# An eight-expert layer with its routing computed during the work: rows' transposes on more PSUM buffers, constant products in the first expert's waits, a fifth raw weight buffer, low parts of weights ahead of routing, and other modelled latencies for the second routing

## The chip, the cores and the metric

One core of a Trainium2 chip. The time is the device time of one execution in microseconds. The kernel before ran three times: 911.78, 912.67 and 908.16, median 911.78. The profile is of a further execution that took 908.89, with a span of 907.0 from its first to its last instruction.

## What is computed

An attention of 4 x 8 heads over 576 positions (windowed in half of the heads, dilated in the others) gives x, 2304 rows of 512. Two layers of experts follow, each with 8 experts of 512 x 1024 and 1024 x 512 weights. All inputs and the output are float32.

```
# first layer: a row goes to one expert, experts take at most 288 rows, best scores first
cap = N // E
for idx in np.argsort(-(x @ w_gate).flatten()):
    tok, e = idx // E, idx % E
    if assigned[tok] >= 0 or counts[e] >= cap: continue
    assigned[tok] = e; counts[e] += 1
for e in range(E): out[mask] = np.maximum(x[mask] @ w1[e], 0.0) @ w2[e]
# second layer: noisy gate, the two best experts of each row, their outputs weighted and summed
noisy_logits = logits + np.log1p(np.exp(x @ w_noise)) * noise
out[mask] += top2_w[mask, k] * (np.maximum(x[mask] @ w1[e], 0.0) @ w2[e])
```

The first layer's assignment is a sequential rule, so the kernel finds one expert's rows after another: it fixes the experts in the order in which they fill, and while it computes expert k it works out who goes to expert k+1 and those behind it.

## The kernel before, in words

**Number format.** Every float32 product of the experts is three products of rounded parts: high x high, low x high, high x low (`mm3`, the line L786). ScalarE rounds an operand to its high part, VectorE subtracts to get the low part. For weights that is `split` (ScalarE `whi` L747 of 128 x 1024, VectorE `wlo` L751 in two halves of 512), for rows `split_x` (`xh` L769, `xl` L770), for the hidden layer `split_h` (`hh` L773, `hl` L774).

**An expert of the first layer.** Its routing list is turned into row numbers (L701 on TensorE, `cp` and `idx` on VectorE). GpSimd gathers 3 x 96 rows `g` from `xr`, the copy of x in DRAM (`gather1`, L796). `tx1` transposes the rows in four groups of three (L810, tiles of the PSUM pool `tr`, which has two buffers) and splits each group into `xh` and `xl`: the third group can't start before the first group's `xl` is out of its buffer. `ffn1` then makes 8 blocks of 12 products (128 x 288 each) for the hidden layer and 4 blocks of 24 for the output: 192 products an expert. After an expert, `post1` computes the second layer's gate from its output (L848), transposes the output back (L867) and writes it to the second layer's x.

**Weights** stream in chunks of 512 KB into the pool `rp` of 4 raw buffers (SyncE issues, L729 for the first matrix, L739 for the second); a raw buffer comes free when the last `wlo` half is subtracted. `load()` issues a chunk when fewer than 4 lie between loaded and split.

**Routing** is a Python generator (`routing`, L451 to L633). For an expert it makes two or three searches for a threshold: VectorE `I` (L540, thresholds against scores), TensorE `OH` products (L558), VectorE `sat` (L560), a small product (L569), `w` (L573); then `choices` (some 20 small VectorE instructions, L491 to L511) and the list. In this text "the sat" is L560.

**The order.** Engines work in program order, and Python sets that order in `build()`: a planner walks through the 192 products of each expert and keeps modelled clocks, `self.pe` for TensorE, `self.dv` for VectorE and `self.tR` for the routing's next TensorE step. `step()` emits the routing's next piece, `spend(t)` advances over a product and emits what has become due, `idle()` emits what is next where the first expert has nothing to compute. `shade(dur)` emits, while VectorE would wait for the routing's answer, what fits: pending `hl` (`self.work`), then low parts of weights through `lows(t, end)`, then routing work of a later expert. `later` holds `hl` back, `flush` empties the queue.

**First expert.** `rows` (L440) transposes x itself, 18 blocks of 128 rows with four transposes each (L446), through the same two `tr` buffers, ScalarE copies the block (L448), SyncE writes it to `xr`. `ROWS0` says how many blocks stand between the routing's steps.

**Second routing.** `noisy` (L879) finds the two best experts of 18 columns of rows: MAX and index instructions in three groups of six (L909, L911), the exponential of the weights on ScalarE (L920, behind a table load), scans (L924), prefix products on TensorE (L928 to L930, called NOISY here), and more VectorE work. `slots` (L991) then builds the list of rows: R (L1014), A (L1023) on VectorE, and products on TensorE (L1028, called SLOT); `gather2` and `tx2` (L1060) bring the rows. It runs once in expert 6 for the rows of experts 0 to 5, and once in the first expert of the second layer.

The calls that matter, with the part that fixes a position: at the end of each first-layer expert `build` finishes what is left of the previous one's `tail`, and for expert 6 that tail holds NOISY and SLOT:

```
                if tail:
                    finish(tail)
                tail = self.post1(k)
                if k == E - 3:
                    tail = itertools.chain(tail, self.noisy(0, NA), first())
```

Of the kernel before, what the change touches and what calls it, by code (L numbers as in the profile page):

```python
# [9 lines left out]
F32 = mybir.dt.float32  # L10
# [14 lines left out]
GB = 96  # L25
# [5 lines left out]
CAP2 = CB * 128  # L31
SEGS = ((0, 256), (256, 384))
# [15 lines left out]
ROWS0 = {False: (6, 1, 3, 1, 3, 1, 3), True: (4, 1, 2, 1, 2, 1, 2, 1, 2, 1, 1)}  # L48
# [97 lines left out]
class Body:  # L146
# [281 lines left out]
    def open_moe(self):  # L428
        tc = self.tc
        self.wp = self.ctx.enter_context(tc.tile_pool(name="wp", bufs=10))  # L430
        self.rp = self.ctx.enter_context(tc.tile_pool(name="rp", bufs=4))
        self.gp = self.ctx.enter_context(tc.tile_pool(name="gp", bufs=5))
        self.yp = self.ctx.enter_context(tc.tile_pool(name="yp", bufs=3))
        self.wk = self.ctx.enter_context(tc.tile_pool(name="wk", bufs=1))
        self.w2 = self.ctx.enter_context(tc.tile_pool(name="w2", bufs=2))
        self.mm = self.ctx.enter_context(tc.tile_pool(name="mm", bufs=4, space=PSUM))
        self.tr = self.ctx.enter_context(tc.tile_pool(name="tr", bufs=2, space=PSUM))
        self.rt = self.ctx.enter_context(tc.tile_pool(name="rt", bufs=2, space=PSUM))

    def rows(self, x0T, c0, c1, psum, name, pool):  # L440

        nc = self.nc
        for c in range(c0, c1):
            ps = psum.tile([128, 512], F32, name=name)
            for kk in range(4):
                nc.tensor.transpose(ps[:, kk * 128:(kk + 1) * 128], x0T[kk][:, c * 128:(c + 1) * 128], self.ident)  # L446
            r = pool.tile([128, XW], F32, name="g")
            nc.scalar.activation(r[:, :DM], ps, AF.Copy)  # L448
            nc.sync.dma_start(self.xr[c * 128:(c + 1) * 128, :DM], r[:, :DM])

    def routing(self):  # L451
# [82 lines left out]
        for k in range(E - 1):  # L534
# [54 lines left out]
            if listed:  # L589

                emit = self.lister(k, place(pk), True)
                while self.low:
                    t, f = self.low.pop(0)
                    f()
                    self.chain(t + 0.05)
                yield "pe", k, 0.85
                emit()
                self.chain(0.4)
            choices()
# [41 lines left out]
    def shade(self, dur):  # L641

        end = max(self.rdy, self.pe) + dur + HOP[1] + SLACK[self.lead > 1]
        for q in (self.work, None, self.low):
            if q is None:
                self.lows(self.dv, end)
                continue
# [5 lines left out]
    def later(self, t, f):  # L653
# [5 lines left out]
        while len(self.work) > 2:  # L659
            t, f = self.work.pop(0)  # L660
            f()
            self.dv = max(self.dv, self.pe) + t

# [215 lines left out]
    def noisy(self, c0, c1):  # L879
# [27 lines left out]
        for j0 in range(0, n, 6):  # L907
# [4 lines left out]
            yield 0.0, 0.16 * (min(n, j0 + 6) - j0) + 0.4  # L912
# [6 lines left out]
        yield 0.0, 1.6  # L919
        nc.scalar.activation(ww, ww, AF.Exp)  # L920
# [4 lines left out]
        yield 0.0, max(3.0, 1.2 + 0.08 * n)  # L925
# [4 lines left out]
        nc.tensor.matmul(pr[:GB, 256:256 + E], self.ones[:GB, :GB], S[:, n - 1, :], start=True, stop=True)  # L930
        V.tensor_tensor(sw[:, :, 0], ww[:, :, 0], ww[:, :, 1], op=OP.add)
# [33 lines left out]
    def ranks(self, e0, e1):  # L965
# [5 lines left out]
        t = wk.tile([GB, NCOL, E], F32, name="rkt")[:, :, :e1 - e0]  # L971
# [3 lines left out]
        nm = wk.tile([GB, NCOL, E], F32, name="nm")[:, :, :e1 - e0]  # L975
# [127 lines left out]
    def build(self):  # L1103
# [18 lines left out]
        self.pend = []  # L1122

# [53 lines left out]
        def idle():  # L1177

            task = min(bg, key=lambda x: x[0], default=None)
            if task and task[0] <= self.tR:  # L1180
# [35 lines left out]
        def load():  # L1216

            while len(raw) < min(len(self.W) + 4, len(chunks)) and known(len(raw)):
# [30 lines left out]
        for n in ROWS0[self.exact]:  # L1249
            step()  # L1250
            self.rows(x0T, c, c + n, self.tr, "t", self.gp)
            c += n
        assert 0 in experts and c == NT
        load()
        split(1)
        until(ready, 0)
        split(4)
        while self.tR < ready[0]:
            idle()
        tx = start(self.tx1(0))  # L1260
# [223 lines left out]
```

## Time and profile before

| what | value |
|---|---|
| median of 3 runs | 911.78 us (908.16 to 912.67) |
| the profiled execution | 908.89 us, span 907.0 us |
| TensorE (PE) busy | 838.4 us, 92% |
| VectorE (DVE) busy | 518.9 us, 57% |
| ScalarE (ACT) busy | 366.7 us, 40% |
| GpSimd (POOL) busy | 183.6 us, 20% |
| chain of work that ended last | PE 72%, DVE 14%, DMA 5% |
| mean granted TensorE clock | 0.968 |

In rows of the timeline the columns are: start in us, duration in us, engine, line, operation, output<-inputs, partitions x elements and type, number of instructions merged; in brackets the idle time of the engine ahead of it and what released it. A granted clock of 1.00 is 2.4 GHz, 0.50 is 1.2 GHz.

### The profile page before, as it was taken

What the parts mean: (1) busy time and instruction counts of PE and PEld (TensorE: products, weight loads), DVE (VectorE), ACT (ScalarE), POOL (GpSimd) and SP (SyncE); (2) the same over time, 40 slices, a digit from 0 to 9 for tenths busy, and PEclk for the clock granted to TensorE, in tenths of its full rate; (3) what the DMA queues carried; (4) which work ended last, traced back from release to release, by engine and by line L of the source; (5) the groups of instructions that cost most, each with busy time, mean ns of one, the idle gap of its engine ahead of it and who ended that gap; (6) DMA issues with size and microseconds to landing.
All of it is one profiled execution on the core that took longest, in us unless ns stands there. A gap on an engine that the chain in (4) does not pass through costs nothing.

```text
span 907.0 us, 16969 instructions
## 1 busy us (share of the span) xinstructions
PE 838.4 (92%) x6723; PEld 760.1 (84%) x6725; DVE 518.9 (57%) x1540; ACT 366.7 (40%) x669; POOL 183.6 (20%) x154
## 2 busy tenths in 40 slices
PE   6888678889999999799899999999999999999993
PEld 3666578789888999799788989889899898998982
DVE  5986668678997654964675627336364372552300
ACT  1767543444345465365134334334333333433210
POOL 3875101010112100010131220322212222122011
PEclk9999869899999999899999999999999999999997
DMA  9960745356556854365335453644545445343112
GB/s 315 305 182 3 290 132 175 94 164 208 143 193 187 290 146 164 102 192 163 84 66 178 126 110 92 165 92 127 128 94 159 69 137 144 74 152 47 14 24 38
DMA packets 54521, 126.26 MB, mean 139 GB/s; under 512 B 7712, under 2 KB 8992, under 8 KB 53664
## 3 DMA queue, kind: packets, MB, share of 16 engines
q1 hardware_dynamic: 40960, 94.46, 32.6%
q0 software_dynamic: 10496, 25.77, 14.7%
q10 hardware_dynamic: 2976, 4.85, 1.7%
q8 instruction: 55, 0.90, 0.4%
q14 instruction: 34, 0.28, 0.1%
HBM read 100.42 MB, written 24.72 MB: 138 GB/s over the span
## 4 chain that ended last, share of the span: by engine, by line
PE 72%; DVE 14%; DMA 5%; issue 3%; ACT 3%; POOL 1%; ACTq 0%; SPq 0%; POOLq 0%; DVEq 0%
PE m L786 60%; DVE wlo L751 3%; PE o L302 2%; PE t L1060 2%; PE r L558 2%; PE ps L283 1%; DMA g<-xr,idx 1%; DVE hl L774 1%; DVE R L695 1%; DMA raw<-in_w2a_dram 1%; DMA ct<-in_consts_dram 1%; PE t L810 1%; PE t L446 1%; PE s L251 1%; PE t L848 1%
## 5 line engine op out<-in xcount | busy, mean ns | idle before, releaser
L786 PE MATMUL m<-xh,whi 128*128 128x384 f32 (+2 forms) x768 | 237.9, 310 | 0.4 <-DVE hl L774 0.4
L786 PE MATMUL m<-xl,whi 128*128 128x384 f32 (+2 forms) x768 | 236.6, 308 | 0.0
L786 PE MATMUL m<-xh,wlo 128*128 128x384 f32 (+2 forms) x768 | 236.5, 308 | 0.0
L751 DVE TENSOR_TENSOR wlo<-raw,whi 128x512 fp32r<-128x512 f32 x256 | 163.7, 683 | 51.6 <-ACT whi L747 51.4
L774 DVE SCALAR_TENSOR_TENSOR hl<-m,hh 128x256 fp32r<-128x256 f32 (+2 forms) x192 | 89.7, 474 | 150.0 <-ACT hh L773 149.9
L773 ACT ACTIVATE hh<-m 128x256 fp32r<-128x256 f32 (+2 forms) x192 | 81.5, 427 | 178.9 <-PE m L786 175.1
L786 PEld LDWEIGHTS m<-xl,whi 128*128 128x128 f32 x768 | 146.7, 191 | 4.0 <-issue 3.7
L747 ACT ACTIVATE whi<-raw 128x1024 fp32r<-128x1024 f32 x128 | 134.4, 1053 | 36.3 <-DMA raw<-in_w1a_dram 11.0
L786 PEld LDWEIGHTS m<-xh,whi 128*128 128x128 f32 x768 | 146.7, 191 | 1.0 <-DVE hl L774 0.6
L786 PEld LDWEIGHTS m<-xh,wlo 128*128 128x128 f32 x768 | 146.3, 191 | 0.5 <-issue 0.5
L786 PE MATMUL m<-whi,hl 128*128 128x512 f32 x320 | 129.1, 403 | 0.5 <-DVE hl L774 0.5
L786 PE MATMUL m<-wlo,hh 128*128 128x512 f32 x320 | 125.5, 392 | 0.0
L786 PE MATMUL m<-whi,hh 128*128 128x512 f32 x320 | 125.3, 392 | 0.0
L1097 POOL DMA_INDIRECT out_dram<-y,tk x40 | 64.0, 1600 | 277.7 <-ACT y L1096 255.0
L1096 ACT ACTIVATE y<-m,wte 128x512 f32<-128x512 f32 x40 | 27.5, 688 | 144.6 <-issue 93.9
L770 DVE TENSOR_TENSOR xl<-t,xh 128x512 fp32r<-128x512 f32 (+1 forms) x72 | 41.8, 586 | 72.9 <-ACT xh L769 72.7
L786 PE MATMUL m<-hl,whi 128*128 128x288 f32 x256 | 79.9, 312 | 2.6 <-DVE hl L774 2.5
L786 PE MATMUL m<-hh,whi 128*128 128x288 f32 x256 | 79.0, 308 | 3.5 <-DVE hl L774 3.5
L786 PE MATMUL m<-hh,wlo 128*128 128x288 f32 x256 | 78.6, 307 | 0.0
L1046 POOL DMA_INDIRECT g<-x,pos x40 | 38.8, 971 | 177.8 <-issue 125.3
L786 PEld LDWEIGHTS m<-wlo,hh 128*128 128x128 f32 x320 | 60.5, 189 | 12.6
L786 PEld LDWEIGHTS m<-whi,hl 128*128 128x128 f32 x320 | 60.6, 189 | 12.5 <-DVE hl L774 1.4
(219 smaller groups left out, 1068.2 us busy)
## 6 DMA issues: line engine op xcount, KB each, us to landing
raw<-in_w1a_dram SPq DMA_DIRECT2D x32, 512.0 KB, 4.4
raw<-in_w2a_dram SPq DMA_DIRECT2D x32, 512.0 KB, 3.9
raw<-in_w1b_dram SPq DMA_DIRECT2D x32, 512.0 KB, 4.4
raw<-in_w2b_dram SPq DMA_DIRECT2D x32, 512.0 KB, 3.7
qt<-in_q_dram SPq DMA_DIRECT2D x8, 576.0 KB, 7.5
kt<-in_k_dram SPq DMA_DIRECT2D x8, 576.0 KB, 8.3
xr<-g SPq DMA_DIRECT2D x18, 256.0 KB, 2.6
x<-y ACTq DMA_DIRECT2D x24, 192.0 KB, 2.2
```

Source lines behind the costliest of these rows:

```text
L302: nc.tensor.matmul(o[r, jj * 64:(jj + 1) * 64], VT[g][:, j, hh * 64:hh * 64 + 64], sb[:, a, half(h ^ i)], start=True, stop=True)
L558: nc.tensor.matmul(pc[:, :E], I[:, :, c], OH[:, c, :], start=c == 0, stop=c == NT - 1)
L747: nc.scalar.activation(hi, raw, AF.Copy)
L751: self.pend.append((chunk, self.pe + LOW[0], lambda s=s: nc.vector.tensor_tensor(lo[:, s], raw[:, s], hi[:, s].bitcast(F32), op=OP.subtract)))
L770: self.nc.vector.tensor_tensor(xl, ps, xh.bitcast(F32), op=OP.subtract)
L773: self.nc.scalar.activation(hh, ps, AF.Relu)
L774: self.later(0.4, lambda: self.nc.vector.scalar_tensor_tensor(hl, ps, 0.0, hh.bitcast(F32), op0=OP.max, op1=OP.subtract))
L786: self.nc.tensor.matmul(ps, a, b, start=i == 0, stop=i == n - 1)
L1046: nc.gpsimd.indirect_dma_start(out=g[:, :DM], out_offset=None, in_=self.x1[:rows, :], in_offset=bass.IndirectOffsetOnAxis(ap=pos[:, b:b + ...
L1060: nc.tensor.transpose(ps[:, kk * 128:(kk + 1) * 128], g[:, kk * 128:(kk + 1) * 128], self.ident)
L1096: nc.scalar.activation(y, ps, AF.Copy, scale=wt[:, b:b + 1])
L1097: nc.gpsimd.indirect_dma_start(out=self.out, out_offset=bass.IndirectOffsetOnAxis(ap=tok[:, b:b + 1], axis=0), in_=y, in_offset=None, comp ...
```

## The change

It has six parts. (1) `rows` takes its PSUM tiles from the four-buffer pool `mm` for two blocks of three and from `tr` for the third, and `ROWS0` deals the blocks out as 3, 1, 4, 1, 4, 1, 4 instead of 6, 1, 3, 1, 3, 1, 3. (2) `fill` issues products of the constant table `thr` (128 x 512, bf16) to a PSUM tile that nobody reads, where the planner sees TensorE wait in the first expert; the order has 5 of them ahead of the first prefix products (L519), 13 ahead of the first list's products (L701), 15 ahead of the search behind it (L558), and 5 ahead of the first `tx1`. (3) `rp` has 5 buffers instead of 4, and `load` runs one chunk further ahead; the tiles `rkt` and `nm` share the buffers of `x1T` and `gp`. (4) Pending `hl` are emitted ahead of `choices`. (5) In `shade`, where the routing is two experts ahead or more, every low part whose high part is due by then is emitted, not only what fits into the wait. (6) In `noisy` the modelled latency of a MAX group is 0.6 per column instead of 0.16, that of the scans 2.8 + 0.08 per column, and the exponential stands behind the prefix products, with a latency of 1.8 of its own.

```
-ROWS0 = {False: (6, 1, 3, 1, 3, 1, 3), ...}
+ROWS0 = {False: (3, 1, 4, 1, 4, 1, 4), ...}
-        self.rp = self.ctx.enter_context(tc.tile_pool(name="rp", bufs=4))
+        self.rp = self.ctx.enter_context(tc.tile_pool(name="rp", bufs=RAW))      # RAW = 5
...
-            ps = psum.tile([128, 512], F32, name=name)
+            ps = self.mm.tile([128, 512], F32, name="m") if c % 3 else self.tr.tile([128, 512], F32, name="t")
...
+            self.flush(False)
             choices()
...
-                self.lows(self.dv, end)
+                self.lows(self.dv, end if self.lead < 2 else 1e9)
...
+    def fill(self, t):
+        n = int(0.8 * min(t, 8.0) / 0.225)
+        if n > 1:
+            x = self.thr.rearrange("p a c -> p (a c)")
+            ps = self.mm.tile([128, 512], F32, name="m")
+            for _ in range(n):
+                self.nc.tensor.matmul(ps, x[:, :128], x[:, :512], start=True, stop=True)
...
-            yield 0.0, 0.16 * (min(n, j0 + 6) - j0) + 0.4
+            yield 0.0, 0.6 * (min(n, j0 + 6) - j0) + 0.4
...
-        yield 0.0, 1.6
-        nc.scalar.activation(ww, ww, AF.Exp)
...
-        yield 0.0, max(3.0, 1.2 + 0.08 * n)
+        yield 0.0, 2.8 + 0.08 * n
         pr = self.rt.tile([128, 512], F32, name="r")
...
+        nc.scalar.activation(ww, ww, AF.Exp)
+        yield 0.1, 1.8
         V.tensor_tensor(sw[:, :, 0], ww[:, :, 0], ww[:, :, 1], op=OP.add)
...
-        t = wk.tile([GB, NCOL, E], F32, name="rkt")[:, :, :e1 - e0]
+        t = wk.tile([GB, NCOL, E], F32, name="rkt", tag="x1T")[:, :, :e1 - e0]
-        nm = wk.tile([GB, NCOL, E], F32, name="nm")[:, :, :e1 - e0]
+        nm = wk.tile([GB, NCOL, E], F32, name="nm", tag="gp")[:, :, :e1 - e0]
...
         def idle():
             task = min(bg, key=lambda x: x[0], default=None)
+            if self.cold:
+                self.fill(min(self.tR, task[0] if task else 1e9) - self.pe)
...
-            while len(raw) < min(len(self.W) + 4, len(chunks)) and known(len(raw)):
+            while len(raw) < min(len(self.W) + RAW, len(chunks)) and known(len(raw)):
...
+        self.cold = not self.exact
...
+        if self.cold:
+            self.fill(ready[0] - self.pe)
+            self.cold = False
```

Because the planner's clocks move, so do instructions of all experts. Where a step stands among TensorE's expert products, as expert.product (0.182 is the 182nd of expert 0's 192; experts 8 and on are the second layer's), counted from the order before and now:

| step | before | now |
|---|---|---|
| tx1 of expert 1, first group | 0.182 | 0.182 |
| last sat's OH products, then tx1, for expert 2 | 1.118, 1.130 | 1.149, 1.165 |
| the same for expert 3 | 2.136, 2.158 | 2.104, 2.113 |
| the same for expert 4 | 3.51, 3.97 | 3.71, 3.97 |
| list products, then tx1, for expert 3 | 2.115, 2.158 | 2.63, 2.113 |
| list products, then tx1, for expert 5 | 4.12 (searches done), 4.97 | 4.65, 4.117 |
| NOISY, SLOT in expert 6 | 6.117, 6.190 | 6.174, 7.0 |
| NOISY, SLOT in the second layer's first expert | 8.67, 8.125 | 8.75, 8.139 |
| SLOT in the second layer's next expert, its tx2 | 9.51, 9.83 | 9.47, 9.83 |

(The row for expert 5 before names the list of expert 5 itself; the searches behind it had ended in expert 3.) Three places in the order are shown, each before and now; the line numbers of the changed kernel are 12 higher there (`wlo` L751 is L763, `xl` L770 is L782, `hl` L774 is L786).

**VectorE in expert 1, from a sat (L560, now L561) of the routing to the rows of expert 2** (`wlo` low parts of weights, `w` and `I` the next search's inputs, `xl` the rows' low parts). Before:

```order
L560 TENSOR_SCALAR sat<-r 64x8
L564 SCALAR_TENSOR_TENSOR wd<-w_1513,dd 128x18
L751 TENSOR_TENSOR wlo<-raw,whi 128x512
L573 TENSOR_SCALAR w_2833<-wd,r 128x18
L540 TENSOR_TENSOR I<-thr,w_2833 128x2304
L751 TENSOR_TENSOR wlo<-raw,whi 128x512 x2
L770 TENSOR_TENSOR xl<-t,xh 128x288 x2
L560 TENSOR_SCALAR sat<-r 128x8
L564 SCALAR_TENSOR_TENSOR wd<-w_2833,dd 128x18
L751 TENSOR_TENSOR wlo<-raw,whi 128x512
L770 TENSOR_TENSOR xl<-t,xh 128x288
L751 TENSOR_TENSOR wlo<-raw,whi 128x512
```

Now:

```order
L561 TENSOR_SCALAR sat<-r 64x8
L565 SCALAR_TENSOR_TENSOR wd<-w_1513,dd 128x18
L763 TENSOR_TENSOR wlo<-raw,whi 128x512 x6
L574 TENSOR_SCALAR w_2917<-wd,r 128x18
L541 TENSOR_TENSOR I<-thr,w_2917 128x2304
L763 TENSOR_TENSOR wlo<-raw,whi 128x512 x2
L782 TENSOR_TENSOR xl<-t,xh 128x288 x4
L561 TENSOR_SCALAR sat<-r 128x8
L565 SCALAR_TENSOR_TENSOR wd<-w_2917,dd 128x18
L763 TENSOR_TENSOR wlo<-raw,whi 128x512 x2
L574 TENSOR_SCALAR w_3036<-wd,r 128x18
L541 TENSOR_TENSOR I<-thr,w_3036 128x2304
```

Six halves of `wlo` stand between the sat and `w` where one stood, and all four `xl` behind them, `I` and two more halves.

**VectorE in expert 6, around the rows of expert 7 and the second routing** (`nzs` its scratch, L909 and L911 now L921 and L923, the scans L924 now L934). Before:

```order
L774 SCALAR_TENSOR_TENSOR hl_5083<-m,hh_5082 128x288
L909 MAX nzs<-nzs 96x8 x6
L911 MAX_INDEX nzs<-nzs 96x8 x6
L751 TENSOR_TENSOR wlo<-raw,whi 128x512 x2
L774 SCALAR_TENSOR_TENSOR hl_5083<-m,hh_5082 128x288
L913 TENSOR_TENSOR nzs<-nzs,ct 96x288
L916 TENSOR_TENSOR mem<-nzs 96x144
L917 TENSOR_TENSOR nzs<-nzs 96x18
L918 TENSOR_TENSOR nzs<-nzs 96x18
L774 SCALAR_TENSOR_TENSOR hl_5083<-m,hh_5082 128x288
L770 TENSOR_TENSOR xl<-t,xh 128x288
L924 SCALAR_TENSOR_TENSOR nzs<-mem 96x18 x8
```

Now:

```order
L786 SCALAR_TENSOR_TENSOR hl_5127<-m,hh_5126 128x288 x2
L782 TENSOR_TENSOR xl<-t,xh 128x288 x4
L921 MAX nzs<-nzs 96x8 x6
L923 MAX_INDEX nzs<-nzs 96x8 x6
L763 TENSOR_TENSOR wlo<-raw,whi 128x512 x4
L925 TENSOR_TENSOR nzs<-nzs,ct 96x288
L928 TENSOR_TENSOR mem<-nzs 96x144
L929 TENSOR_TENSOR nzs<-nzs 96x18
L930 TENSOR_TENSOR nzs<-nzs 96x18
L934 SCALAR_TENSOR_TENSOR nzs<-mem 96x18 x8
L763 TENSOR_TENSOR wlo<-raw,whi 128x512 x4
L943 TENSOR_TENSOR nzs<-nzs 96x18
```

The four `xl` stand ahead of the third MAX group instead of behind it, and eight halves of `wlo` ahead of the work that follows the prefix products (L943, before L931).

**ScalarE in expert 6, the exponential and its table load** (L920, now L941; `x1T` is the expert's output). Before:

```order
L773 ACTIVATE hh_5082<-m 128x288 x3
L769 ACTIVATE xh<-t 128x288
L920 ACT_TABLE_LOAD
L920 ACTIVATE nzs<-nzs 96x36
L769 ACTIVATE xh<-t 128x288
L747 ACTIVATE whi<-raw 128x1024
```

Now:

```order
L851 ACTIVATE x1T<-m 128x288
L759 ACTIVATE whi<-raw 128x1024
L851 ACTIVATE x1T<-m 128x288
L759 ACTIVATE whi<-raw 128x1024
L851 ACTIVATE x1T<-m 128x288
L941 ACT_TABLE_LOAD
L941 ACTIVATE nzs<-nzs 96x36
L851 ACTIVATE x1T<-m 128x288
```

The load and the exponential stood between the first and second `xh`; they stand between the third and the fourth `x1T`.

## Rows read from the trace of the kernel before

**Rows 1.** What PE waits for, whole span: engine, line, releaser, total us, times, longest us

```profile
PE t L810 <- DVE xl L770: 9.6, 3, 4.6
PE m L786 <- DVE hl L774: 6.9, 6, 2.9
...
PE r L1028 <- DVE A L1023: 3.9, 2, 2.4
```

**Rows 2.** Windows A:B in us: length, busy us by engine, granted clock, DMA share, GB/s

```profile
108.40:128.90 20.50, 11.52 (x77) 10.38 (x77) 12.74 (x43) 9.14 (x15) 3.49 (x3) 0.50 0.72 225
...
129.00:159.00 30.00, 27.07 (x232) 25.83 (x230) 25.00 (x80) 9.55 (x16) 2.78 (x3) 1.00 0.43 140
143.00:146.00 3.00, 1.71 (x13) 1.71 (x14) 1.97 (x6) 2.32 (x3) 0.00 (x0) 1.00 0.97 371
...
367.90:374.70 6.80, 5.93 (x28) 5.88 (x29) 5.49 (x22) 4.05 (x11) 0.00 (x0) 0.50 0.27 83
...
446.30:449.80 3.50, 3.50 (x15) 2.79 (x12) 0.48 (x4) 0.00 (x0) 1.88 (x2) 0.51 0.82 193
```

**Rows 3.** Timeline of PE, the dummy products at the start

```profile
12.51 1.89 PE L370 MATMUL ps<-wz 128*128 128x512 bf16 x8 [0.16 <-issue]
```

**Rows 4.** Timeline of PE, first expert: prefix and list products, search, first expert product

```profile
104.31 0.18 PE L519 MATMUL r<-EQ,tri 128*128 128x36 bf16 x1
...
106.43 2.15 PE L701 MATMUL r<-A,R 128*96 128x6 bf16 x18 [1.91 <-DVE R L695]
112.01 1.28 PE L558 MATMUL r<-OH,I 128*128 128x8 bf16 x18 [3.43 <-DVE I L540]
...
121.64 0.59 PE L786 MATMUL m<-xh,whi 128*128 128x288 f32 x1
```

**Rows 5.** Timeline of DVE, expert 0, from a sat to the rows of expert 1

```profile
154.71 2.48 DVE L751 TENSOR_TENSOR wlo<-raw,whi 128x512 fp32r<-128x512 f32 x4
157.12 0.23 DVE L573 TENSOR_SCALAR w<-wd,r 128x18 bf16<-128x18 f32 x1
157.38 1.36 DVE L540 TENSOR_TENSOR I<-thr,w 128x2304 bf16<-128x2304 bf16 x1
...
161.81 0.82 DVE L770 TENSOR_TENSOR xl<-t,xh 128x288 fp32r<-128x288 f32 x2 [1.88 <-ACT xh L769]
```

**Rows 6.** Timeline of PE: two expert products, the rows of expert 1, a wait in expert 1

```profile
137.90 0.30 PE L786 MATMUL m<-xh,whi 128*128 128x288 f32 x1
138.03 0.29 PE L786 MATMUL m<-xl,whi 128*128 128x288 f32 x1
...
162.33 0.74 PE L810 MATMUL t<-ct,g 96*128 96x96 f32 x3 [4.52 <-DVE xl L770]
...
186.87 0.59 PE L786 MATMUL m<-hh,whi 128*128 128x288 f32 x1 [2.88 <-DVE hl L774]
```

**Rows 7.** Timeline of PE, expert 2: list products of expert 3, then its last gathered rows

```profile
230.85 0.28 PE L701 MATMUL r<-A,R 128*96 128x6 bf16 x3
...
241.10 0.30 PE L810 MATMUL t<-ct,g 96*128 96x96 f32 x1 [0.72 <-DMA g<-xr,idx]
```

**Rows 8.** Timeline of ACT and of PE, expert 6: exponential, rows, NOISY, SLOT

```profile
363.33 1.28 ACT L920 ACT_TABLE_LOAD   x1
368.01 0.23 ACT L920 ACTIVATE nzs<-nzs 96x36 f32<-96x36 f32 x1 [3.40 <-DVE nzs L918]
...
368.77 0.74 PE L810 MATMUL t<-ct,g 96*128 96x96 f32 x3 [4.55 <-DVE xl L770]
...
372.77 0.32 PE L928 MATMUL r<-mem,tri 96*96 96x144 bf16 x1
...
385.25 0.60 PE L1028 MATMUL r<-A,R 96*128 96x21 bf16 x18 [1.59 <-DVE A L1023]
```

**Rows 9.** Timeline of DVE, expert 6, behind NOISY: first and last of the work ahead of SLOT

```profile
373.06 0.17 DVE L931 TENSOR_TENSOR nzs<-nzs 96x18 f32<-96x18 f32 x1
...
384.82 0.37 DVE L1023 TENSOR_TENSOR A<-Ab,W 96x162 bf16<-96x162 f32 x1
```

More of the change, by code (lines that the diff above doesn't have):

```diff
@@ L31 @@
 CAP2 = CB * 128
+RAW = 5
 SEGS = ((0, 256), (256, 384))
@@ L47 @@
 LOAD = (3.0, 5.0)
-ROWS0 = {False: (6, 1, 3, 1, 3, 1, 3), True: (4, 1, 2, 1, 2, 1, 2, 1, 2, 1, 1)}
+ROWS0 = {False: (3, 1, 4, 1, 4, 1, 4), True: (4, 1, 2, 1, 2, 1, 2, 1, 2, 1, 1)}
 WARM = (14, 2, 9)
@@ L438, in open_moe, with rows @@
         self.rt = self.ctx.enter_context(tc.tile_pool(name="rt", bufs=2, space=PSUM))
-    def rows(self, x0T, c0, c1, psum, name, pool):
+    def rows(self, x0T, c0, c1, pool):
         nc = self.nc
         for c in range(c0, c1):
-            ps = psum.tile([128, 512], F32, name=name)
+            ps = self.mm.tile([128, 512], F32, name="m") if c % 3 else self.tr.tile([128, 512], F32, name="t")
             for kk in range(4):
@@ L1250, in build @@
             step()
-            self.rows(x0T, c, c + n, self.tr, "t", self.gp)
+            self.rows(x0T, c, c + n, self.gp)
             c += n
@@ L1259, in build @@
             idle()
+        if self.cold:
+            self.fill(ready[0] - self.pe)
+            self.cold = False
         tx = start(self.tx1(0))
```

## The prediction

> **What bounds the kernel now.** I read the shares first, then what TensorE waits for over the whole span, then the granted clock in windows, then the timeline of each wait, and last the two orders side by side. TensorE is busy 92% of the span, so a change pays only where TensorE stands still or runs at half clock. The list of its waits is short [rows 1]: 9.6 us on the rows' low parts `xl`, 6.9 on `hl`, 3.9 on the table A of the second routing. The reader is to see that VectorE ends most of them though it is busy 57% of the span: what counts is the order on VectorE in a few stretches. From 129 to 159 us it is busy 25.0 of 30 us [rows 2].
>
> Each long wait has a second price. The granted clock is 0.50 or 0.51 around the first expert and behind the waits that end at 368.77 and 445.70 [rows 2, 8], and 1.00 across a wait of 1.3 us (143 to 146, TensorE busy 1.71 of 3.00) [rows 2]. A product of 288 columns takes 0.131 us at full clock [rows 6]. Half clock for 3.5 us behind a wait of 2.4 [rows 1, 2] does 1.75 us of work, so it costs 1.75; behind the 4.55 wait it is 5.93 busy us, so 2.95.
>
> **The change, part by part.** Sums are against the profiled execution, 908.9 us, which is 2.9 below the median of the runs. Where the order puts a step is given as expert.product, as in the table of the change.
>
> *First expert.* Eight dummy products took 1.89 us [rows 3], 0.236 each. The five ahead of L519 stand on the path: L519 starts right behind the transposes, and its answer leads to the list [rows 4]. So +1.1; nothing if the more evenly dealt blocks end that much earlier, +2.2 if they run at half clock. The 13 behind them, 3.1 us, lie beside VectorE's R: TensorE waits 1.91 for its first table, and its list products then take 2.15 because the tables come one by one [rows 4]; behind the dummies they find them made. The 15, 3.5 us, lie beside `I`, for which it waits 3.43 [rows 4]. The last five stand behind that search, where gathers are awaited. I cost these at nothing; at half clock, twice as long, they would add some 4. The four-buffer pool saves waits of the transposes on ScalarE copies, a quarter microsecond each, which the same path swallows.
>
> *Rows of expert 1.* Before, the stop of 4.52 us [rows 6] ends when VectorE gets `xh` late, after idling 1.88 [rows 5]. With a fifth raw buffer ScalarE isn't held by a weight load there, but eight halves of `wlo` now follow the sat instead of four. From the sat just ahead of 154.6 on: 8 x 0.605 (four take 2.41 up to `w` [rows 5]) = 4.8, `w` 0.25, `I` 1.36, one `xl` 0.41: 161.4 instead of 162.3, so -0.9. With the dummies +0.2 in all. If neither the load nor the dummies matter it is -0.9; if the fifth load takes bandwidth from the gather, +2.
>
> *Rows of experts 2, 3 and 4.* This is the term that decides. The third group of transposes needs the first `xl` out. From the sat to that `xl` VectorE has, in expert 1, eight halves, `w`, `I` and one `xl`: 4.8 + 0.25 + 1.36 + 0.41 = 6.8; TensorE has 19 products and two groups, 19 x 0.131 + 0.8 (a group with its reload about 0.4, half of the 0.74 at half clock [rows 6]) = 3.3. It stops for 3.5; I take 3.2, as the planner's earlier `hl` leave VectorE a little ahead. In expert 2: two `hl` 0.8, six halves 3.6, `w`, `I`, `xl`: 6.4 against 10 products and two groups, 2.1: 4.2. In expert 3: 6.9 with one `hl` more, against 29 products and two groups, 4.6: 2.4. Together 9.8. In return the wait on `hl` in expert 1 goes (2.9 [rows 6]), as `hl` now stand ahead of `choices`; so does the wait for gathered rows in expert 2 (0.7 [rows 7]), since TensorE waits longer for something else; of the other 4.0 on `hl` [rows 1] I give 1.8 back. 9.8 - 5.4 = +4.4. Bounds: 0 if all halves had been done by then, since their raw buffers come sooner, and +6 if nothing is given back.
>
> *Rows of expert 5.* Its list moves from 4.12 to 4.65, and `tx1` is at 4.117. From list products to the last gathered group it took 241.10 - 230.85 = 10.25 [rows 7]; now 52 products (6.8), the list itself (18 short products, three take 0.28 [rows 7], so under 1) and two ready groups give 8.1. So +2.1 (0 to +2.5), at the cost of no other wait before.
>
> *Clock behind these waits.* Three or four stops of 2 to 4 us where there was one of 2.9: between no extra stretch at half clock and two extra (+3.5); I take one, +1.75.
>
> *Second routing in expert 6.* Before, ScalarE holds its second `xh` behind an exponential that waits 3.40 for VectorE, and TensorE stops for 4.55 [rows 8]. That goes: TensorE is at 364.2 at 6.105, and but for 0.5 us goes on. 69 products and two groups later it is at NOISY (6.174): 364.2 + 0.5 + 9.0 + 0.8 = 374.5, against 372.77 [rows 8]. The exponential, now behind the third `x1T` (6.168), ends near 373.8 + 0.4 + 1.28 + 0.23 = 375.7. From L931 to A VectorE took 12.1 us [rows 9] with two pairs of `wlo` among it, 1.2 each by [rows 5]: 9.7 without them. A is ready at 385.4; the third MAX group and eight halves ahead of it may make it 1.7 later, and I take 1.0: 386.4, against 385.25. TensorE reaches SLOT, at the expert's end, at 377: it has 18 products (2.4 us) behind NOISY where it had 73. So it stands some 9 us there; the 4.55 and its half clock are spent in this one wait instead. SLOT is 1.2 later, and the clock falls behind it (1.75 to 2.95, I take 2.3), where it didn't behind 1.59: +3.5, bounds +2 and +6.
> The Trainium skill, "ScalarE: Activation LUTs", section "What ACT_TABLE_LOAD costs", gives a table switch about 2.66 us, with a drain behind the load; the trace shows a load of 1.28 and no drain apart. By the page the exponential would end 1.4 later, and the sum would be 1.3 higher; I stay with the row.
>
> *Second routing in the second layer.* NOISY moves 8 products later, SLOT 14, that is about 3.2 us of products in that stretch by 0.23 each (0.236 for a product as wide [rows 3]); A comes some 1.3 later, so the wait of 2.4 shrinks to about 0.5, and the 1.75 of half clock behind it [rows 1, 2] goes: -3.5 (-4.2 to 0). SLOT of the next expert stands 4 products of about 0.2 earlier, and so its gathers, for which TensorE waits: -0.8.
>
> Shared tiles and modelled clocks cost nothing by themselves: `rkt` is used when no `x1T` is live.
>
> **Sum:** 0.2 + 4.4 + 2.1 + 1.75 + 3.5 - 3.5 - 0.8 = +7.7, 916.6 for an execution like the profiled one, 919.5 on top of the median. Forecast: **918**, by its own bounds 912 to 925.
>
> **Rivals.** *Low parts early are simply early (faster).* With `wlo` ahead, later work on VectorE is lighter; if by the sat of experts 1 to 3 no half is left to do, the stretch up to `xl` is 2 us and the waits there vanish: -5.4 for +4.4, the clock's extra 1.75 goes and the 1.7 behind 2.9 us comes back, and the stop at 162.33 loses 2 of its 4.5. 0.2 - 2 - 5.4 - 1.7 + 0 + 3.5 - 3.5 - 0.8 = -9.7: about 899 to 902. For it: a buffer more lets SyncE load earlier, and VectorE is idle 43% of the whole. Against: it is busy 83% in just this stretch [rows 2], and the order puts the halves behind the sat. It decides where fewer than three halves remain there. Chance 0.20.
> *The moves cancel:* the waits of experts 1 to 3 come out near the 5.4 that they replace, expert 6 pays 2 and the second layer gives 3.5 back: 909 to 912. For it: every term above is a wait exchanged for another. Chance 0.16.
> *The dummies hold the clock.* It is 0.50 from 108.4 to 128.9 [rows 2], and the first expert's products start at 121.64 [rows 4]: 7.3 us at half clock, worth 3.6. If filled waits kept it at 1.00 to there, the forecast falls by 3.6 to some 914. Against: behind the search only five dummies and the rows' transposes stand until 121.6, whatever is filled before; of 108.4 to 121.6 TensorE had work for 4.2 us (11.52 less 7.3) [rows 2]. Chance 0.12. The Trainium skill's "TensorE: Matmul & The Clock Gate", section "What's actually happening", says that activity releases the throttle and idling brings it back; by that rule the products would help if they reached far enough, and the trace agrees so far that the clock falls behind waits.
> *Both routings late.* If the exponential or the eight halves slip by some 5 us, SLOT in expert 6 does too, and it is 927 or more. Chance 0.05.
>
> **How the numbers follow.** The forecast's case has 0.47. The range, **904 to 925**, leaves out most of the first rival and the last one. About 0.5%, 4.5 us, is what a measurement of this kernel can tell from no change: bounds 907.2 and 916.3 around the median. Slower by more: 0.87 of the forecast's case and the last rival, 0.46. Faster by more: the first rival and a little of the second, 0.22. The rest, 0.32, is the same.
>
> **What would show it.** In the waits of TensorE: on `xl` still near 10 us or above, but in experts 1 to 3 rather than 0 and 6; one wait on A of 7 to 10 us at the end of expert 6; less than 1 us on A in the second layer; `hl` under 4 us. Gate to gate, expert 2 grows most. Right for another reason if the first expert's product starts 3 us later. The forecast is wrong if waits on `xl` fall under 5 us in all, or the wait on A in expert 6 is under 4.

## The result, and the profile after

The changed kernel takes 922.52 us, the median of 4 runs (921.29 to 924.96), against 910.42 for the kernel before beside it (4 runs). The ratio is 1.0136, with a 95% interval of 1.0100 to 1.0172: slower by some 12 us. Its profiled execution took 924.96 (span 923.2), 16.1 more than that of before; it is the slowest of its four, as the one of before is near its fastest, so some 4 us of these 16 lie between executions.

What TensorE waits for in the changed kernel, whole span, in the columns of [rows 1]:

```profile
PE t L822 <- DVE xl L782: 15.8, 6, 4.7
PE r L1040 <- DVE A L1035: 9.9, 2, 8.4
PE t L822 <- DMA g<-xr,idx: 5.2, 6, 2.3
...
PE m L798 <- DVE hl L786: 2.9, 4, 1.4
...
PE r L559 <- DVE dg L543: 1.8, 1, 1.8
PE t L1072 <- DVE xl L782: 1.4, 1, 1.4
```

Against [rows 1], `hl` falls from 6.9 to 2.9, `xl` rises from 9.6 to 15.8 and A from 3.9 to 9.9. The fifth line is a wait that didn't exist before: the first expert's first search waits for its inputs from VectorE.

Next the first expert on TensorE, where [rows 4] stood:

```profile
91.22 0.60 PE L447 MATMUL t<-ct,x 128*128 128x128 f32 x4
91.66 1.04 PE L447 MATMUL m<-ct,x 128*128 128x128 f32 x8
94.47 1.25 PE L559 MATMUL r<-OH,I 128*128 128x8 bf16 x18 [1.77 <-DVE dg L543]
...
111.52 1.40 PE L713 MATMUL r<-A,R 128*96 128x6 bf16 x18
112.78 3.40 PE L674 MATMUL m<-thr 128*128 128x512 bf16 x15
116.35 1.28 PE L559 MATMUL r<-OH,I 128*128 128x8 bf16 x18 [0.17 <-DVE I L541]
...
121.36 0.42 PE L822 MATMUL t<-ct,g 96*128 96x96 f32 x1 [1.14 <-DMA g<-xr,idx]
...
125.89 0.59 PE L798 MATMUL m<-xh,whi 128*128 128x288 f32 x1
```

The dummies do cover the waits on R and `I` (1.91 and 3.43 in [rows 4], none and 0.17 here). But the list starts 20.3 us after the first transposes where it started 16.5 after them (from 89.97), and TensorE still waits for gathered rows (1.14).

Then the stops at the rows of experts 1 to 5 and at SLOT of expert 6, where [rows 6 to 8] stood (rows of one timeline; the last is the SLOT of the second layer's first expert):

```profile
167.45 0.74 PE L822 MATMUL t<-ct,g 96*128 96x96 f32 x3 [4.70 <-DVE xl L782]
...
205.47 0.47 PE L822 MATMUL t<-ct,g 96*128 96x96 f32 x3 [2.96 <-DVE xl L782]
...
238.76 0.47 PE L822 MATMUL t<-ct,g 96*128 96x96 f32 x3 [3.39 <-DVE xl L782]
...
274.21 0.50 PE L822 MATMUL t<-ct,g 96*128 96x96 f32 x3 [1.84 <-DVE xl L782]
...
317.36 0.30 PE L822 MATMUL t<-ct,g 96*128 96x96 f32 x1 [2.34 <-DMA g<-xr,idx]
...
381.70 0.47 PE L822 MATMUL t<-ct,g 96*128 96x96 f32 x3 [2.41 <-DVE xl L782]
...
402.60 0.63 PE L1040 MATMUL r<-A,R 96*128 96x21 bf16 x18 [8.44 <-DVE A L1035]
...
465.42 0.75 PE L1040 MATMUL r<-A,R 96*128 96x14 bf16 x24 [1.46 <-DVE A L1035]
```

And the granted clock (the column behind POOL's, as in [rows 2]) of the first transposes, of the first expert, and behind four of these stops:

```profile
96.20:104.00 7.80, 7.80 (x56) 7.67 (x56) 3.47 (x7) 4.78 (x8) 0.00 (x0) 0.56 0.56 207
...
121.00:124.00 3.00, 1.30 (x5) 0.82 (x6) 0.92 (x2) 0.00 (x0) 0.00 (x0) 0.50 0.86 208
...
205.40:208.90 3.50, 3.43 (x19) 3.42 (x20) 1.30 (x4) 1.11 (x5) 0.00 (x0) 0.62 1.05 401
...
238.70:243.00 4.30, 4.24 (x25) 4.24 (x26) 1.28 (x4) 2.06 (x6) 0.00 (x0) 0.69 0.94 329
274.00:278.00 4.00, 3.79 (x18) 3.57 (x19) 2.16 (x6) 2.06 (x6) 0.00 (x0) 0.57 0.56 198
...
402.60:410.00 7.40, 7.40 (x59) 6.12 (x59) 0.78 (x5) 3.27 (x6) 2.87 (x3) 0.66 0.41 110
```

Each of these stretches is mostly at 1.2 GHz. The first is new: before, the same transposes ran at 1.00. The same window of the kernel before, counted from its first transposes:

```profile
95.00:102.80 7.80, 7.48 (x78) 6.38 (x77) 4.06 (x13) 4.81 (x9) 0.00 (x0) 1.00 0.79 293
```

Not every stop is followed by half clock: behind the one of 2.41 (381.70) the granted clock is 1.00 from 381 to 386.

Where the 16 us came in is read from a few points of the program on TensorE: the first of the rows' transposes, the first list products (L701), the first gate product of each expert (L848), and the end. The columns "list" and "expert 0" count from the first transposes; "1 to 5" and "6, 7" are the stretches between gates; "rest" runs from the last gate to the end. All are us of one profiled execution each. The part ahead of the first transposes, identical in all, differs by up to 4 us between executions. Up to the gate of expert 0, before, only_noisy and noisy_free run the same instructions and take 74.3, 72.9 and 72.4, so a difference of 2 us in that column shows nothing by itself.

| kernel | start | list | expert 0 | 1 to 5 | 6, 7 | rest |
|---|---|---|---|---|---|---|
| before | 90.0 | 16.5 | 74.3 | 182.6 | 69.2 | 490.9 |
| the change | 91.2 | 20.3 | 78.2 | 192.6 | 72.8 | 488.4 |
| only_rows | 88.6 | 17.4 | 74.8 | 182.8 | 69.1 | 490.8 |
| only_fill | 89.1 | 18.3 | 70.7 | 183.3 | 69.2 | 490.3 |
| only_lows | 91.9 | 16.5 | 75.1 | 197.1 | 70.7 | 491.5 |
| only_noisy | 89.4 | 16.5 | 72.9 | 183.0 | 72.8 | 488.2 |
| fill_raw5 | 90.0 | 18.4 | 73.1 | 184.4 | 69.1 | 491.6 |
| fill_rows | 89.3 | 21.4 | 75.4 | 183.5 | 69.1 | 490.8 |
| all_but_lows | 91.6 | 17.7 | 73.8 | 182.8 | 74.1 | 488.6 |
| lows_flush | 90.5 | 16.5 | 76.6 | 195.2 | 69.2 | 491.3 |
| noisy_free | 92.5 | 16.5 | 72.4 | 182.4 | 65.9 | 488.8 |
| after_free | 92.0 | 17.8 | 76.4 | 191.0 | 68.5 | 492.1 |
| fill_free | 89.9 | 18.3 | 72.8 | 183.4 | 67.3 | 487.7 |
| fill_free_raw | 90.4 | 18.3 | 74.3 | 185.4 | 67.2 | 490.3 |

For the change: +1.2 ahead of the rows, +3.9 in expert 0, +10.0 in experts 1 to 5, +3.6 in 6 and 7, -2.5 in the second layer: 16.2.

### The profile page after: what moved, and what is told of

It reads as the page before. It is cut to its first block, busy times and chain, and to the rows that moved or that the text cites. A ratio compares the mean times of both kernels' runs of the same rounds, so it can differ in the third digit from the quotient of the medians.

```text
span 923.2 us, 17054 instructions
## 1 busy us (share of the span) xinstructions
PE 851.0 (92%) x6763; PEld 770.0 (83%) x6763; DVE 519.7 (56%) x1540; ACT 367.4 (40%) x669; POOL 184.0 (20%) x154
## 4 chain that ended last, share of the span: by engine, by line
PE 77%; DVE 10%; DMA 6%; ACT 3%; issue 2%; POOL 1%; SPq 0%; ACTq 0%; POOLq 0%; DVEq 0%
PE m L798 63%; DVE wlo L763 3%; PE r L559 2%; PE o L303 2%; PE t L1072 2%; PE ps L284 1%; DMA g<-xr,idx 1%; PE t L879 1%; DMA ct<-in_consts_dram 1%; DVE hl L786 1%; PE t L822 1%; DMA mask<-in_masks_dram 1%; DVE R L707 1%; DMA kt<-in_k_dram 1%; PE s L252 1%
## 5 line engine op out<-in xcount | busy, mean ns | idle before, releaser
L763 DVE TENSOR_TENSOR wlo<-raw,whi 128x512 fp32r<-128x512 f32 x256 | 162.2, 682 | 51.1 <-ACT whi L759 50.9
L786 DVE SCALAR_TENSOR_TENSOR hl<-m,hh 128x256 fp32r<-128x256 f32 (+2 forms) x192 | 89.1, 474 | 145.2 <-ACT hh L785 144.9
L782 DVE TENSOR_TENSOR xl<-t,xh 128x512 fp32r<-128x512 f32 (+1 forms) x72 | 41.7, 586 | 72.3 <-ACT xh L781 72.3
L1058 POOL DMA_INDIRECT g<-x,pos x40 | 38.7, 967 | 182.6 <-issue 98.6
L808 POOL DMA_INDIRECT g<-xr,idx x24 | 24.4, 1015 | 239.6 <-DVE hl L786 72.5
```

The costliest lines, as they stand in the source:

```text
L763: self.pend.append((chunk, self.pe + LOW[0], lambda s=s: nc.vector.tensor_tensor(lo[:, s], raw[:, s], hi[:, s].bitcast(F32), op=OP.subtract)))
L782: self.nc.vector.tensor_tensor(xl, ps, xh.bitcast(F32), op=OP.subtract)
L786: self.later(0.4, lambda: self.nc.vector.scalar_tensor_tensor(hl, ps, 0.0, hh.bitcast(F32), op0=OP.max, op1=OP.subtract))
L808: nc.gpsimd.indirect_dma_start(out=g[:GB], out_offset=None, in_=self.xr, in_offset=bass.IndirectOffsetOnAxis(ap=self.IDX[k][:, j:j + 1], a ...
L1058: nc.gpsimd.indirect_dma_start(out=g[:, :DM], out_offset=None, in_=self.x1[:rows, :], in_offset=bass.IndirectOffsetOnAxis(ap=pos[:, b:b + ...
```

## The experiments

Ratios are to runs of the kernel before on the same chip. The first four kernels each hold one part of the change alone, as its diff has it; the shared tiles of part 3 (`rkt`, `nm`) stand in every kernel here. Parts 3 and 4 were not run alone: part 3 is added to the dummies, part 4 to part 5.

**Part 5 alone (low parts without the limit).**

```
-                self.lows(self.dv, end)
+                self.lows(self.dv, end if self.lead < 2 else 1e9)
```

> The kernel before with part 5 alone (low parts of weights without the limit of the wait, where the routing is two experts ahead); the rows' dealing, dummies, fourth raw buffer, choices and second routing as before. Theory: the order of VectorE behind the sat costs the time, so experts 1 to 4 take about 9 us more from gate to gate in the profile, as they do in the whole change (there 9.1), TensorE waits about 3, 3.5 and 2 us on xl in experts 1 to 3, and the median is 7 to 11 us above before. Rival: those waits come from the fifth buffer's loads or the dummies, and this run is within 3 us of before.

Measured: 926.64, ratio 1.0184 (1.0130 to 1.0239). It is 17.7 above, more than the whole change: the theory's mechanism, but I had the size from the whole change, whose other parts give some of it back. Experts 1 to 5 take 14.5 more. The stops on `xl` are 3.93 and 1.85 in experts 1 and 2; in expert 3 TensorE waits 2.65 on `hl` instead. The order differs too: alone, the list of expert 5 stands at 4.89 instead of the change's 4.65. Waits of TensorE:

```profile
PE t L821 <- DVE xl L781: 17.6, 7, 5.5
PE m L797 <- DVE hl L785: 8.1, 8, 2.7
```

With `hl` not ahead of `choices`, those waits stay, on top of the new ones on `xl`.

**Part 6 alone (second routing).** The diff's lines in `noisy`.

> The kernel before with part 6 alone (latencies of the second routing and the place of the exponential). Theory: in expert 6 the wait of 4.6 us on xl shrinks to 2.5 or less, one of about 8.5 us on A appears at its end, and expert 6 and 7 together take 3.7 us more; in the second layer the wait on A shrinks by 1 and about 2.5 us come back: the median 0 to 2.5 us above before. Rival: the wait on A comes from the low parts put ahead of it by part 5, which is absent here, then expert 6 is faster than before by 4 us or more and the median 4 to 8 us below.

Measured: 908.94, ratio 1.0001 (0.9979 to 1.0023), as the theory has it: experts 6 and 7 lose 3.6, the second layer gives 2.7 back. The low parts of part 5 aren't there, and the wait on A is the same 8.4:

```profile
PE r L1039 <- DVE A L1034: 9.9, 2, 8.4
PE t L821 <- DVE xl L781: 6.7, 3, 3.8
```

**Part 2 alone (dummies).**

> The kernel before with part 2 alone (38 dummy products in the first expert's waits). Theory: only the five ahead of the prefix products are on the path, so the first expert product starts 1.1 us later and the clock is 0.50 there as before: the median 0.5 to 2 us above before. Rival: the dummies hold the clock at 1.00 through the first products: 2 to 4 us below.

Measured: 906.18, ratio 0.9975 (0.9951 to 0.9999): the rival's side, 2.7 faster, though only just clear of no change. The list starts 1.8 later, of which 0.7 is caught up within its products, so the five dummies do cost some 1.1. But the first expert product comes 1.4 earlier from the first transposes, and in the profiled execution at full clock. Its timeline of TensorE:

```profile
112.24 1.28 PE L559 MATMUL r<-OH,I 128*128 128x8 bf16 x18 [0.17 <-DVE I L541]
...
116.97 1.17 PE L821 MATMUL t<-ct,g 96*128 96x96 f32 x6
...
119.38 0.38 PE L797 MATMUL m<-xh,whi 128*128 128x288 f32 x1
119.60 0.29 PE L797 MATMUL m<-xl,whi 128*128 128x288 f32 x1
```

In a window of the same kernel from there on, the clock is 1.00:

```profile
119.40:124.00 4.60, 4.09 (x41) 3.81 (x40) 3.50 (x9) 2.87 (x7) 0.00 (x0) 1.00 0.39 126
```

But the dummies didn't hold the clock through: it had fallen, and the last five dummies ran at half clock. The stretch ahead of the first `tx1`:

```profile
114.90:118.30 3.40, 3.24 (x12) 1.65 (x11) 2.97 (x5) 1.47 (x3) 0.00 (x0) 0.50 0.71 221
```

What the dummies do is to make the clock fall later: the fall ahead of the first expert's products comes 25 to 31 us after the first transposes in all eight kernels with dummies, and 16 to 19 after them in the six without. That it was back at 1.00 at the first product is seen in this profile alone.

No wait for gathered rows is left in the first expert. Issued 1 us later beside the same four loads of weights, the gathers land after 4.4 us (median of three) instead of 7.0.

**Part 1 alone (rows).**

> The kernel before with part 1 alone (blocks dealt 3, 1, 4, 1, 4, 1, 4, tiles from two pools). Theory: three more transposed blocks stand between the steps of the first search, which is on the path to the first list, so the first list's products start about 2 us later: the median 1.5 to 3 us above before. Rival: the waits of the transposes on ScalarE that the second pool saves make up for it, within 1 us.

Measured: 910.29, ratio 1.0017 (0.9995 to 1.0038), between the two and not clear of no change; the list starts 0.9 later. The mechanism isn't the one expected. Three blocks ahead of the first search instead of six leave TensorE waiting 1.78 us for `choices` and the search's inputs on VectorE, and the clock falls in the transposes behind it. The timeline of TensorE, and a window:

```profile
91.88 1.25 PE L559 MATMUL r<-OH,I 128*128 128x8 bf16 x18 [1.78 <-DVE dg L543]
```

```profile
94.00:98.00 4.00, 4.00 (x32) 3.95 (x32) 1.37 (x2) 2.65 (x5) 0.00 (x0) 0.59 0.55 207
```

**Dummies with the fifth buffer, and with the rows.** Parts 2 and 3, and parts 1 and 2, to see why the whole change has its first product at half clock.

> Parts 2 and 3 (dummies and the fifth raw buffer), all else as before; only_fill was 906.2 with the clock at 1.00 from the first expert product on. Theory: the fifth buffer's load runs beside the gathers of the first rows, which land about 7 us after issue instead of 4.4, TensorE waits for them, the clock is 0.50 at the first product as in the whole change: 908 to 911. Rival: the later rows of part 1 do that, and this run keeps the clock: 905 to 907.

> Parts 1 and 2 (blocks dealt otherwise and dummies), all else as before. Theory that the fifth buffer delays the gathers: the gathers land as early as in only_fill, the clock is 1.00 at the first product, and the time is that of only_fill plus 1 to 2, 906.5 to 908.5. Rival, that the later rows delay them: they are awaited by 2 us or more, the clock is 0.50 there, and the time is 909 to 911.

Measured: 909.65 (1.0023, 1.0000 to 1.0047) and 912.01 (1.0039, 1.0016 to 1.0062). The first is in its theory's bracket; the second is above both of its brackets. Each undoes what the dummies gave, so neither theory excludes the other. With the fifth buffer its load is issued at 109.03 instead of 114.76, just ahead of the gathers (111.09), TensorE waits for them in three pieces, and the first product is at half clock. The timeline of SyncE's queue and of TensorE:

```profile
109.03 16.35 SPq L750 DMA_DIRECT2D raw<-in_w2a_dram  x4
...
118.69 0.39 PE L821 MATMUL t<-ct,g 96*128 96x96 f32 x1 [0.63 <-DMA g<-xr,idx]
...
122.46 0.59 PE L797 MATMUL m<-xh,whi 128*128 128x288 f32 x1
```

With the rows, the same 1.78 us wait at the first search is followed by 9 us at half clock, and the list starts 21.4 us after the first transposes:

```profile
94.00:103.00 9.00, 9.00 (x57) 8.54 (x56) 3.66 (x10) 4.78 (x8) 0.00 (x0) 0.50 0.48 177
```

TensorE waits only 0.27 us for the gathers there, where the rival asked for 2 or more: it is the list that is late, 3.1 behind that of only_fill, and the first product is 2.9 behind.

**The whole change without part 5.**

> The whole change without part 5 (the limit of the wait is back for low parts). Theory: part 5 carries the loss, so the waits on xl in experts 1 to 3 are under 1 us each, the search products are back where they were, and the time falls by 11 to 18 from 922.5 to between 905 and 912. Rival: the parts share the loss about evenly, and it stays above 915.

Measured: 916.23, ratio 1.0093 (1.0057 to 1.0130), in the bracket that I gave the rival. The table says how: experts 1 to 5 are back at 182.8, so the 10 us there are part 5's; but experts 6 and 7 take 74.1 here and the gathers are awaited for 5.5 us. The profile shows too little of what is left: it took 912.77, the other three runs 915.5 to 917.0, at mean granted clocks of 0.962 to 0.966 instead of 0.972. By the medians, each beside its own before, leaving part 5 out takes back only 5.1 of the 12.1 us. Part 5 is the largest share seen, not the whole.

**The second routing's list not forced to the end of expert 6**, on part 6 alone and on the whole change:

```
-        tail = None
+        tail = slow = None
...
-                if nl == 8 and tx is None and k + 1 == E and tail not in bg:
+                if nl == 8 and tx is None and k + 1 == E and tail not in bg and slow not in bg:
...
-                if tail:
+                if k == E - 2:
+                    slow = tail
+                elif tail:
                     finish(tail)
...
+        finish(slow)
         finish(tail)
```

> Part 6 alone, and the builder no longer forces the list products of the second routing to the end of expert 6: the order puts them at 7.61 instead of 7.0. Theory: the wait of 8.4 us on A comes from that place alone, so it falls under 1 us, with the half clock behind it; the xl wait of 3.8 stays or shrinks: 5 to 8 us below only_noisy's 908.9, 901 to 904. Rival: VectorE's work behind the prefix products is late anyway and the wait moves along, or returns as a wait for gathered rows at 7.108: within 2 us of only_noisy.

> The whole change, and the builder no longer forces the second routing's list products to the end of expert 6. Theory: as with part 6 alone, where that gave 4 us, the wait of 8.4 us on A falls under 2 us: 4 to 6 us below the change's 922.5, 916.5 to 918.5. Rival: inside the whole change VectorE is later by the low parts, and the wait returns at the new place: within 2 us of 922.5.

Measured: 905.11 (0.9962, 0.9939 to 0.9985) and 919.17 (1.0092, 1.0059 to 1.0125). Both lie between theory and rival: part 6 is 3.8 below only_noisy where 5 to 8 were expected. Experts 6 and 7 take 65.9 instead of 72.8, and 68.5 in the whole change; the wait on A is 1.34 us, and the clock behind it stays at 1.00. noisy_free's timeline of TensorE, and a window:

```profile
391.69 0.60 PE L1039 MATMUL r<-A,R 96*128 96x21 bf16 x18 [1.34 <-DVE A L1034]
```

```profile
392.00:398.00 6.00, 6.00 (x56) 6.00 (x53) 4.50 (x12) 1.78 (x4) 3.29 (x3) 1.00 0.62 217
```

So it was the place of SLOT that turned the later NOISY into an 8.4 us stop. In the whole change the medians are 3.4 apart, a little less than expected: waits for gathered rows of the second layer take 4.2 us there and 0.9 in the change.

**Parts 4 and 5.**

> Parts 4 and 5 alone (low parts without the limit, hl ahead of choices), all else as before; part 5 alone gave 926.6, 17.7 above before. Theory: flush brings the lists of experts 4 to 6 back by 24 to 56 products and takes the hl waits away, so experts 1 to 5 take what they take in the whole change, 9 to 11 more than before: 918 to 921. Rival: part 4 does nothing and it stays at 925 or above.

Measured: 923.03, ratio 1.0141 (1.0111 to 1.0170), between the theories. Part 4 helps (the lists stand where the whole change has them, `hl` is down to 3.4 us), but experts 1 to 5 still take 12.6 more, 2.6 above the whole change. The fifth buffer, absent here, would be the candidate: waits on `xl` are 20.7 here and 15.8 there. No run adds it to these two parts. But beside the dummies it shortens the stop at the rows of expert 1 from 3.90 (only_fill) to 2.48 (fill_raw5), and in the pair at the end of this section from 3.78 to 2.55.

**The best of it.** Parts 2 and 6 with SLOT unforced, then the same with a fifth buffer that was meant to wait:

```
-            while len(raw) < min(len(self.W) + RAW, len(chunks)) and known(len(raw)):
+            while len(raw) < min(len(self.W) + (RAW if len(self.W) > 4 else 4), len(chunks)) and known(len(raw)):
```

> Parts 2 and 6 (dummies, second routing's latencies and exponential), list products not forced to the end of expert 6, all else as before. Theory: the two gains are in different stretches and add: 2.7 of only_fill and 4.1 of noisy_free, so 901 to 903.5 beside a before of 909. Rival: they overlap, or the clock at the first product is only full by luck of that run: 904 to 907.

> As fill_free, with the fifth raw buffer used only once the first expert's four chunks of the first matrix are split, so that no fifth load runs beside its gathers. Theory: the clock stays full at the first product as in only_fill, and the wait on xl at the rows of expert 1 shrinks from about 4 to 2.5 as in fill_raw5: 0.5 to 2 us below fill_free. Rival: the load's place doesn't matter, the loads collide elsewhere: 0 to 2 above fill_free.

Measured: 901.15, ratio 0.9930 (0.9900 to 0.9960), the lowest of all; and 906.39 (0.9969, 0.9947 to 0.9992), 5.2 above it and so outside both brackets. The two gains of the first add. In its profile the first product is at half clock (0.50 from 116.0 to 123.0, with no wait for rows), so the full clock of only_fill is not to be counted on, and the half clock of fill_raw5 can't be put down to the fifth load. The rows that come without a wait are the same in both profiles. The second edit missed its aim: with four chunks split the limit allows eight, a fifth buffer is free, and the load still went out at 109.47, ahead of the gathers, with TensorE waiting 2.32 for them. A fifth buffer that really starts later wasn't tried.

## Why the prediction was right, point by point

The forecast was +7.7, 918, between 904 and 925; measured were +12.1 in the medians and 16.1 between profiles. The sign, the range and the mechanism held; the size fell short by 4 to 8. Of the 8.5 us between the sum and the two profiles 3.7 lie in the first expert, 1.8 in experts 1 to 5 (the clock behind the waits), 1.8 in the second layer and 1.2 ahead of the first transposes.

*Rows of experts 2 to 5.* Forecast were stops of 3.2, 4.2 and 2.4, then 2.1 for the rows of expert 5; measured 2.96, 3.39, 1.84 and 2.34. VectorE's timeline ahead of the first of them shows the eight halves in front of `xl`:

```profile
198.62 3.68 DVE L763 TENSOR_TENSOR wlo<-raw,whi 128x512 fp32r<-128x512 f32 x6
...
203.76 1.29 DVE L763 TENSOR_TENSOR wlo<-raw,whi 128x512 fp32r<-128x512 f32 x2
204.97 0.81 DVE L782 TENSOR_TENSOR xl<-t,xh 128x288 fp32r<-128x288 f32 x2
```

(The 10.25 us in the step for expert 5 counts from the last three list products, with which [rows 7] begins; the 18 begin at 230.20, which makes it 10.9.) TensorE's idle time between the gates of experts 0 and 5 (span less busy time in those windows) went from 6.1 to 12.2 us: +6.1 where the terms gave 4.4 + 2.1. The term that was too small is the clock's: I took one extra stretch at half clock, 1.75. All four stops have one, where before had two, and TensorE's busy time there rose by 3.9 us with the same products. The second of before I had not read, and it stands behind no wait: ahead of it TensorE was busy all the time, in part with the 36 short products of a search and a list.

```profile
226.00:231.30 5.30, 5.28 (x61) 5.11 (x59) 5.16 (x20) 2.30 (x3) 0.00 (x0) 1.00 0.00 0
231.30:234.70 3.40, 3.40 (x14) 3.14 (x15) 3.33 (x12) 0.48 (x2) 1.05 (x2) 0.50 0.73 177
```

One reading failed though it cancels in the sum: I expected expert 2 to grow most, but experts 1 to 3 together take 1.6 less and expert 4 takes 10.6 more, since three searches (18 products, 1.28 us each) and a list moved into it, some 4.8 us, and its wait and half clock come on top.

*Second routing in expert 6.* Forecast +3.5 with a wait of 9; measured 8.44 and +3.6 over experts 6 and 7. From the first VectorE instruction behind NOISY to A it took 9.8 us (9.7 forecast). The timelines of ScalarE and VectorE:

```profile
391.23 1.28 ACT L941 ACT_TABLE_LOAD   x1
392.52 0.23 ACT L941 ACTIVATE nzs<-nzs 96x36 f32<-96x36 f32 x1
...
392.79 0.17 DVE L943 TENSOR_TENSOR nzs<-nzs 96x18 f32<-96x18 f32 x1 [1.13 <-ACT nzs L941]
...
402.18 0.37 DVE L1035 TENSOR_TENSOR A<-Ab,W 96x162 bf16<-96x162 f32 x1
```

Here TensorE reached NOISY at 391.39, and the exponential began 0.01 us behind its table load and took 0.23. The Trainium skill, "ScalarE: Activation LUTs", "What ACT_TABLE_LOAD costs", gives 2.66 us for a switch, drain included. These rows show 1.28 and no drain between the load and the exponential, so the row's price was the right one. The `xl` stop shrank to 2.41, not 0.5: two `hl` and a MAX group stand ahead of `xl`.

*Rows of expert 1.* Forecast -0.9, measured +0.2 (4.70 for 4.52): the last two of the eight halves waited 0.93 us for `whi`, which the sum took as ready. The fifth buffer does help here: without part 5 (all_but_lows) the stop is 2.55, so the halves cost 2.15 of the 4.70. VectorE's timeline:

```profile
159.58 3.68 DVE L763 TENSOR_TENSOR wlo<-raw,whi 128x512 fp32r<-128x512 f32 x6
164.19 1.29 DVE L763 TENSOR_TENSOR wlo<-raw,whi 128x512 fp32r<-128x512 f32 x2 [0.93 <-ACT whi L759]
...
166.95 0.81 DVE L782 TENSOR_TENSOR xl<-t,xh 128x288 fp32r<-128x288 f32 x2
```

*First expert.* This step failed in size: forecast +0.2 to the rows of expert 1, measured +3.9. The five dummies were priced rightly. The other thing, that re-dealing the blocks is swallowed, was wrong: fewer blocks ahead of the first search open a 1.77 us wait there, and 7.8 us of transposes follow at 0.56. only_rows shows that wait and the clock without the rest, fill_rows with the dummies. all_but_lows and after_free run the same instructions there and have the same wait with the clock at 1.00, and their lists start 2.5 earlier than the change's: so the drop comes in some executions only. That the fifth load makes TensorE wait for the first gathers, which I had only as a bound at the rows of expert 1, is shown by fill_raw5. I had named as a sign of being right for another reason that the first product starts 3 us later. It does: 34.67 after the first transposes, 31.67 before. So the 3.9 us of this step have another reason than the forecast's. The sign and the range don't rest on them: experts 1 to 7 alone lose 13.6, of which the second layer gives 2.5 back.

*Second layer.* Forecast -4.3, measured -2.5: the wait on A is 1.46 instead of 0.5, though without half clock behind it, and 1.39 on `xl` in `tx2` is new. The sign "less than 1 us on A" failed with it.

*Rivals.* That the dummies hold the clock (0.12) is half true: they make it fall 7 us later or more, but at the first product it was at 1.00 in only_fill alone, not in the change; what they gave alone goes with either of parts 1 and 3 beside them. That early low parts are simply early is excluded by only_lows, that the moves cancel by the result itself, and that both routings come late by SLOT in expert 6, which cost the forecast's 3.5.

## What to carry to other kernels

A low-priority work item that is put ahead of a latency chain delays everything that hangs on the chain, however idle its engine is on average: give it the gaps, and keep the limit on what fits in one. A builder that forces a step to be done at some point turns a more honest latency into a wait there; move the deadline together with the latency. A short wait has to be priced with the half clock that may follow it, and a load that is started early should be looked at beside the transfer that something waits for.

## What the runs showed that was not expected

The length of one wait didn't tell whether the clock falls. Behind the wait of 1.8 us at the first search, with the same instructions around it, 1.2 GHz followed in three of five profiles of kernels with part 1 (0.56, 0.59 and 0.50 over 4 to 9 us; 1.00 in the other two). Behind waits of 1.38 (143 to 146 in [rows 2]), 1.34 (noisy_free) and even 2.41 (expert 6 of the change) the clock stayed at 1.00; in only_fill it fell right behind one of 1.25, and at 231 in the kernel before with no wait ahead at all.

The first three gathers took 7.0 us from issue to landing before, 4.4 in only_fill, where they were issued 1 us later after the first transposes, and 7.1 in the whole change, with the weights' loads beside them: issued later, the rows came earlier. This is one pair of profiles, and that the later issue is the reason isn't shown.
